# Attention scores copied to SBUF by the maximum, masks one and transposes two iterations later

## The chip, the cores and the metric

One core of a Trainium2 chip. The metric is the device time of one execution in microseconds (us), the median of three runs of the kernel before: 988.97 (988.1 to 991.67). Engines: PE is TensorE, PEld its weight load, DVE is VectorE, ACT is ScalarE, POOL is GpSimd, SP issues most DMAs.

## The reference, cut to what matters

```
scores = scale * q @ k.T                      # 4 batches x 8 heads, 576 x 576, head size 64
thresh = max(scores, axis=-1) - tau
scores = where(scores >= thresh, scores, -1e9)
attn = exp(scores - max(scores)); attn /= sum(attn) + 1e-9
x = (attn @ v) as [2304, 512]
e = argmax(x @ w_gate + bias); x = gate * (relu(x @ w1[e]) @ w2[e])   # 8 experts, one per token
h = x @ w_in; out = (h * sigmoid(1.702 h)) @ w_out
```

Only the attention is touched by the change.

## The kernel before, in words

The attention works on 16 pairs of heads (4 per batch). A pair is 9 units: unit w < 8 is 128 query rows of one head, unit 8 holds the last 64 rows of both heads. So there are 144 units, and `run` makes two of them in each iteration; nine iterations are two pairs.

Of one unit, in the old code:

- `qk` (L201 to L217): four (unit 8: eight) matmuls on TensorE give scores of 128 x 576 in a PSUM tile `sc`, of which there are two. K and Q are split into a high and a low part, and operand tiles hold both.
- `max` (L219 to L226): a TENSOR_REDUCE on VectorE over `sc` gives the negated maximum `nmx`.
- `thr` (L228 to L232): threshold from `nmx`, on VectorE, from iteration 66 on GpSimd.
- `exp` (L234 to L238): ScalarE, from `sc` in PSUM.
- `mask` (L240 to L271): SCALAR_TENSOR_TENSOR on VectorE: `sc >= thr` times `e`, with the row sum accumulated, into `E`. After unit 8 of every second pair come four small steps for the reciprocals.
- `trans` (L274 to L297): four transposes on TensorE, and a copy on ScalarE to `AT`. `trans_tails` does the last 64 columns.
- `av_items`: 10 pieces for each pair, matmuls with V; `row_items`: 5 pieces for every second pair, which turn the result into rows, scale them on GpSimd (`xrow`, `lgt`) and write them out.

An iteration `it` does units 2it and 2it+1 from `qk` to `mask` and the transposes of the two units before. Each engine takes its work in the order in which it is written. Tables (`AV`, `ROW`, `AVL`, `ROWL`) say how many pieces of `avq` and `rowq` go into an iteration, `sides` puts steps of the router in between, and from iteration 54 (`IT_LAST`) on these steps also stand between the masks.

Operands of pair p+2 are made while pair p runs: `load` (DMA of K and Q), then two pieces of `split` (L144 to L154), one for each iteration, on GpSimd: scale the query half, cast to the high part `kA`, subtract for the low part `kB`. After the second, `place` copies halves of the tiles on the SP queue: four DMAs (L161 to L164).

Of the kernel before, what the change touches and what calls it, by code (L numbers as in the profile page):

```python
# [24 lines left out]
UPP = 9  # L25
# [7 lines left out]
NS0 = 7  # L33
CO = (0, 2)
CA = (0, 1, 2, 2, 2, 2, 2, 2, 2, 2, 2, 2, 2, 2, 2, 2)
# [6 lines left out]
NROW = 2  # L42
IT_THR = 66
SN = 1
# [3 lines left out]
class Attention:  # L48
# [12 lines left out]
    def __init__(self, ctx, late_ctx, tc, kq, v, tau, w_gate, x_dram, router, ident, ps):  # L61
# [9 lines left out]
        self.kp = P("a_k", 3)  # L71
        self.ep = P("a_e", 4)
        self.ex = P("a_exp", 3)
        self.et = P("a_et", 2)
        self.sm = P("a_small", 4)
        router.wk["A"] = P("r_work_a", 1)
# [13 lines left out]
        self.w_gate = w_gate  # L90
        self.qT = [cst.tile([128, 1536], F32R, name=f"qT{i}") for i in range(3)]
        for t in self.qT:
# [39 lines left out]
    def operands(self, p):  # L132
        d = self.st[p]
        d["qT"] = self.qT[p % 3]
        for x in ("kA", "kB"):
            d[x] = self.kp.tile([128, 1536], F32R, name=x)

# [5 lines left out]

    def split(self, p, i, pieces):  # L144

        nc = self.nc
        d = self.st[p]
        n = 640 // pieces
        A, B_, F = (self.heads(d[x], n, i * n) for x in ("kA", "kB", "F"))
# [68 lines left out]

    def max(self, u):  # L219
        nc = self.nc  # L220
        p, w = divmod(u, UPP)
        d = self.st[p]
        sc = d["sc", w]
# [4 lines left out]
    def thr(self, u, eng):  # L228
        p, w = divmod(u, UPP)
        d = self.st[p]  # L230
        d["thr", w] = thr = self.sm.tile([128, 1], F32, name="thr")
        eng.tensor_scalar(thr, d["nmx", w], -1.0, self.taue[:, 0:1], op0=ALU.mult, op1=ALU.subtract)  # L232

    def exp(self, u):  # L234
        p, w = divmod(u, UPP)
        d = self.st[p]
        d["e", w] = e = self.ex.tile([128, 2, 288], F32, name="e")
        self.nc.scalar.activation(e, d["sc", w][:, :, 0:288], ACTF.Exp, bias=d["nmx", w][:, 0:1], scale=1.0)  # L238

    def mask(self, u):  # L240
# [17 lines left out]
        else:  # L258
# [132 lines left out]
    def run(self):  # L391
# [15 lines left out]
        while done < NU:  # L407
            last = it >= IT_LAST
            us = [u for u in (2 * it, 2 * it + 1) if u < NU]
            ts = [u for u in (2 * it - 2, 2 * it - 1) if 0 <= u < NU]  # L410
            starts = [u // UPP for u in us if u % UPP == 0]
            for p in starts:
                if p + 3 < NPAIR:
                    self.load(p + 3)
                if p + 2 < NPAIR:
                    self.load_v(p + 2)
                for n in range(1 if p == 0 else p + 2, min(p + 3, NPAIR)):
                    self.operands(n)
                    self.poolq += [lambda n=n, i=i: self.split(n, i, NPC) for i in range(NPC)]
            thr_eng = nc.gpsimd if it >= IT_THR else nc.vector  # L420
            copies = []
            for i in range(2):
# [4 lines left out]
                if i == 0 and not last:  # L427
                    n = AV1[it % 9]
                    while n and avq:
                        avq.pop(0)()  # L430
                        n -= 1
            for i in range(2):
                for c in range(2):
                    if CO[c] == 2 * i and c < len(copies):
                        copies[c]()
                if i < len(us):
                    self.max(us[i])
                    self.exp(us[i])
                for c in range(2):
                    if CO[c] == 2 * i + 1 and c < len(copies):  # L440
                        copies[c]()
# [10 lines left out]
            n = AVL[it - IT_LAST] if last else AV[it % 9]  # L452
# [5 lines left out]
            n = ROWL[it - IT_LAST] if last else ROW[it % 9]  # L458
# [999 lines left out]
```

## Time and profile before

| what | us |
|---|---|
| median of three runs | 988.97 (988.1 to 991.67) |
| the profiled execution, own time | 989.85 |
| its span, first to last instruction | 988.1 |
| TensorE busy in the span | 932.2 (94%) |
| VectorE busy | 568.2 (58%) |
| ScalarE busy | 440.2 (45%) |
| GpSimd busy | 241.6 (24%) |
| first score matmul, last score matmul | 7.6, 311.7 |

The attention is the first third, from 7.6 to about 320 us; the experts and the last layer follow. Busy shares of the span are means over these stages. In the views, a line's "idle" is the time its engine stood still just before it, and behind the arrow stands what ended it.

### The profile page before, as it was taken

To read this page: it belongs to the slowest core of one execution; us is meant where nothing else is said; L and a number is where in the kernel's file an instruction comes from. 1 tells how busy PE (TensorE), PEld (TensorE's weight loads), DVE (VectorE), ACT (ScalarE), POOL (GpSimd) and SP (SyncE) were. 2 spreads that over 40 slices of the span, in tenths; PEclk is the share of its full clock that TensorE was granted. 3 is DMA by queue.
4 is the path that set the end of the run, shared out by engine and by line. 5 is a ranking of instruction groups with operands and counts; after the bars stand their busy time and mean duration, and the time that the engine had idled before them with its cause. 6 is when DMAs were issued, how large, how long until landed. Compare 5 with 4: busy or idle time off the path is not lost. (4 is left out here: it accounts for less than half of the span.)

```text
span 988.1 us, 14131 instructions
## 1 busy us (share of the span) xinstructions
PE 932.2 (94%) x4991; PEld 747.5 (76%) x4991; DVE 568.2 (58%) x1182; ACT 440.2 (45%) x799; POOL 241.6 (24%) x338
## 2 busy tenths in 40 slices
PE   5799899999987989999999999999999999999994
PEld 4677677777765668777788888888888888888894
DVE  6698999898886387676777569971111111111110
ACT  4567677777665434343444434542222222222221
POOL 5735565666415332020222010010001000100100
PEclk9899999999999999999999999999999999999998
DMA  6766645655504426545645224330011000100000
GB/s 181 176 169 182 147 126 132 155 139 125 125 9 115 149 69 199 193 159 175 204 166 190 72 86 150 106 107 23 1 44 43 1 0 22 43 1 1 33 11 24
DMA packets 78571, 100.08 MB, mean 101 GB/s; under 512 B 28639, under 2 KB 51679, under 8 KB 78496
## 3 DMA queue, kind: packets, MB, share of 16 engines
q1 hardware_dynamic: 74656, 86.63, 30.9%
q0 software_dynamic: 3840, 12.50, 3.8%
q8 instruction: 41, 0.67, 0.3%
q14 instruction: 34, 0.28, 0.1%
HBM read 63.46 MB, written 17.23 MB: 82 GB/s over the span
## 5 line engine op out<-in xcount | busy, mean ns | idle before, releaser
L1154 DVE TENSOR_TENSOR hl<-sg,hh 128x512 fp32r<-128x512 f32 (+1 forms) x80 | 51.0, 638 | 243.1 <-ACT hh L1152 240.4
L1151 ACT ACTIVATE sg<-tr 128x512 f32<-128x512 f32 (+1 forms) x80 | 44.2, 553 | 208.6 <-PE tr L938 205.2
L214 PE MATMUL sc<-kA,qT 128*128 128x288 f32 x320 | 105.5, 346 | 25.4 <-DVE thr L232 8.0
L225 DVE TENSOR_REDUCE nmx<-sc 128x1 f32<-128x576 f32 x144 | 108.4, 753 | 22.1 <-PE sc L214 20.5
L938 PE MATMUL tr<-xh,wi_h 128*128 128x512 f32 (+1 forms) x320 | 120.6, 377 | 0.0
L938 PE MATMUL tr<-xh,wi_l 128*128 128x512 f32 (+1 forms) x320 | 118.8, 371 | 0.0
L938 PE MATMUL tr<-xl,wi_h 128*128 128x512 f32 (+1 forms) x320 | 118.7, 371 | 0.0
L238 ACT ACTIVATE e<-sc,nmx 128x576 f32<-128x576 f32 x144 | 108.0, 750 | 18.4 <-DVE nmx L225 18.1
L960 PE MATMUL sc<-wo_h,hl 128*128 128x512 f32 x288 | 113.8, 395 | 0.0
L960 PE MATMUL sc<-wo_l,hh 128*128 128x512 f32 x288 | 113.7, 395 | 0.0
L960 PE MATMUL sc<-wo_h,hh 128*128 128x512 f32 x288 | 113.5, 394 | 0.0
L262 DVE SCALAR_TENSOR_TENSOR E<-sc,thr,e 128x576 f32<-128x576 f32 x128 | 104.3, 815 | 12.2 <-ACT e L238 8.2
L291 ACT COPY AT<-tr 128x512 f32<-128x512 f32 x128 | 75.0, 586 | 61.1 <-PE tr L289 59.4
L214 PEld LDWEIGHTS sc<-kA,qT 128*128 128x128 f32 x320 | 62.5, 195 | 45.5 <-issue 25.5
L214 PE MATMUL sc<-kB,qT 128*128 128x288 f32 x320 | 92.8, 305 | 1.2 <-DMA kB<-kB 1.1
L289 PE MATMUL tr<-ident,E 128*128 128x128 f32 x512 | 79.7, 280 | 0.2 <-DVE E L262 0.2
L335 PE MATMUL av<-AT,V 128*64 128x288 f32 x512 | 77.0, 420 | 0.0
L938 PEld LDWEIGHTS tr<-xh,wi_l 128*128 128x128 f32 x320 | 60.2, 188 | 11.3
L938 PEld LDWEIGHTS tr<-xl,wi_h 128*128 128x128 f32 x320 | 60.3, 188 | 11.2
L938 PEld LDWEIGHTS tr<-xh,wi_h 128*128 128x128 f32 x320 | 60.2, 188 | 11.2
L960 PE MATMUL sc<-bl,hh 128*128 128x512 f32 x152 | 60.1, 395 | 6.5 <-DVE bl L1179 6.5
L289 PEld LDWEIGHTS tr<-ident,E 128*128 128x128 f32 x512 | 65.0, 145 | 0.8 <-DVE E L262 0.7
(213 smaller groups left out, 1757.3 us busy)
## 6 DMA issues: line engine op xcount, KB each, us to landing
ra<-in_moe_w_dram SPq DMA_DIRECT2D x20, 512.0 KB, 5.2
rb<-in_moe_w_dram SPq DMA_DIRECT2D x20, 512.0 KB, 3.9
F<-in_kq_dram SPq DMA_DIRECT2D x15, 640.0 KB, 5.4
cv_raw<-in_moe_w_in_dram SPq DMA_DIRECT2D x16, 512.0 KB, 4.8
cv_raw<-in_moe_w_out_dram SPq DMA_DIRECT2D x16, 512.0 KB, 3.9
kA<-kA SPq DMA_DIRECT2D x15, 320.0 KB, 3.3
kB<-kB SPq DMA_DIRECT2D x15, 320.0 KB, 3.5
x_dram<-xrow SPq DMA_DIRECT2D x72, 64.0 KB, 2.1
```

Source lines behind the costliest of these rows:

```text
L214: nc.tensor.matmul(sc[:, hf, 0:288], l, d[kk][:, c0 + hf * 288:c0 + (hf + 1) * 288], start=(i == 0), stop=(i == len(ops) - 1),)
L225: nc.vector.tensor_reduce(out=nmx, in_=sc[:, :, 0:288], axis=AX.XY, op=ALU.max, negate=True)
L238: self.nc.scalar.activation(e, d["sc", w][:, :, 0:288], ACTF.Exp, bias=d["nmx", w][:, 0:1], scale=1.0)
L262: nc.vector.scalar_tensor_tensor(out=E.rearrange("p (a c) -> p a c", a=2), in0=d["sc", w][:, :, 0:288], scalar=d["thr", w][:, 0:1], in1=d[ ...
L289: nc.tensor.transpose(tp[:, kc * 128:(kc + 1) * 128], E[:, k0 + kc * 128:k0 + (kc + 1) * 128], self.ident)
L291: copies.append(lambda: nc.scalar.copy(AT[:, h, :, c * 128:(c + 1) * 128], tp.rearrange("p (k c) -> p k c", k=4)))
L335: nc.tensor.matmul(d["av"][h * 64:(h + 1) * 64, 0:288], d["V"][:, h, kc, :], d["AT"][:, h, kc, hf * 288:(hf + 1) * 288], start=False, stop ...
L938: nc.tensor.matmul(hps[:, 0:T], w[:, kd, :], blk[x][:, kd, :], start=(i == 0), stop=(i == 11))
L960: nc.tensor.matmul(y, h[:, cs], w, start=(f == 0 and i == 0), stop=(f == blk["nf"] - 1 and i == 2))
L1151: nc.scalar.activation(sg, hps, ACTF.Gelu_apprx_sigmoid)
L1154: return [upper, lambda: nc.vector.tensor_sub(hl, sg, hh.bitcast(F32))]
```

## The change

- `max` is a TENSOR_SCALAR on VectorE: it writes the negated scores to an SBUF tile `ns` (three of them) and accumulates the minimum of these, which is `nmx`. `exp` and `mask` read `ns` (with the sign turned), and no longer `sc`.
- `thr` is on GpSimd always.
- An iteration does `qk`, `max`, `exp` and `thr` of units 2it and 2it+1, `mask` of the two units before these, and transposes of the two units before those. VectorE's order is mask, maximum, mask, maximum. The tables are read one iteration later (`jt`).
- `split` becomes `high` (scale and cast, GpSimd) and `low` (subtract, VectorE), queued as high, high, low, low, one for each iteration (two in iteration 0). `place` follows the second `low`.
- `load_v` of pair p+2 is issued when unit 0 of pair p is transposed, two iterations later than before.
- One more `E` tile, six instead of four of the small tiles, operand tiles of 1408 instead of 1536 columns.

The core of the diff:

```diff
-    def split(self, p, i, pieces):
+    def high(self, p, i, pieces):
+        nc = self.nc
+        d = self.st[p]
+        n = 640 // pieces
+        A, F = (self.heads(d[x], n, i * n) for x in ("kA", "F"))
+        nc.gpsimd.tensor_scalar_mul(F[64:128], F[64:128], self.cq[64:128, 0:1])
+        nc.gpsimd.tensor_copy(A, F)
+
+    def low(self, p, i, pieces):
         d = self.st[p]
         n = 640 // pieces
         A, B_, F = (self.heads(d[x], n, i * n) for x in ("kA", "kB", "F"))
-        nc.gpsimd.tensor_scalar_mul(F[64:128], F[64:128], self.cq[64:128, 0:1])
-        nc.gpsimd.tensor_copy(A, F)
-        nc.gpsimd.tensor_sub(B_, F, A.bitcast(F32))
+        self.nc.vector.tensor_sub(B_, F, A.bitcast(F32))
         if i == pieces - 1:
             self.place(p)
...
-        nc.vector.tensor_reduce(out=nmx, in_=sc[:, :, 0:288], axis=AX.XY, op=ALU.max, negate=True)
-        d["nmx", w] = nmx
+        ns = self.sn.tile([128, 2, 288], F32, name="ns")
+        nc.vector.tensor_scalar(
+            ns, d["sc", w][:, :, 0:288], -1.0, 3.0e38, op0=ALU.mult, op1=ALU.min, accum_out=nmx)
+        d["nmx", w], d["ns", w] = nmx, ns
...
-        eng.tensor_scalar(thr, d["nmx", w], -1.0, self.taue[:, 0:1], op0=ALU.mult, op1=ALU.subtract)
+        self.nc.gpsimd.tensor_scalar(thr, d["nmx", w], self.taue[:, 0:1], None, op0=ALU.add)
...
-        self.nc.scalar.activation(e, d["sc", w][:, :, 0:288], ACTF.Exp, bias=d["nmx", w][:, 0:1], scale=1.0)
+        self.nc.scalar.activation(e, d["ns", w], ACTF.Exp, bias=d["nmx", w][:, 0:1], scale=-1.0)
...
-            out=E.rearrange("p (a c) -> p a c", a=2), in0=d["sc", w][:, :, 0:288],
-            scalar=d["thr", w][:, 0:1], in1=d["e", w], op0=ALU.is_ge, op1=ALU.mult, accum_out=acc,
+            out=E.rearrange("p (a c) -> p a c", a=2), in0=d["ns", w],
+            scalar=d["thr", w][:, 0:1], in1=d["e", w], op0=ALU.is_le, op1=ALU.mult, accum_out=acc,
...
-            last = it >= IT_LAST
-            us = [u for u in (2 * it, 2 * it + 1) if u < NU]
-            ts = [u for u in (2 * it - 2, 2 * it - 1) if 0 <= u < NU]
+            jt = it - 1
+            last = jt >= IT_LAST
+            us, ms, ts = ([u for u in (2 * n, 2 * n + 1) if 0 <= u < NU] for n in (it, it - 1, it - 2))
...
-                if p + 2 < NPAIR:
-                    self.load_v(p + 2)
                 for n in range(1 if p == 0 else p + 2, min(p + 3, NPAIR)):
                     self.operands(n)
-                    self.poolq += [lambda n=n, i=i: self.split(n, i, NPC) for i in range(NPC)]
+                    self.poolq += [lambda n=n, i=i, f=f: f(n, i, NPC) for f in (self.high, self.low) for i in range(NPC)]
...
             for i in range(2):
-                for c in range(2):
-                    if CO[c] == 2 * i and c < len(copies):
-                        copies[c]()
+                if i < len(copies):
+                    copies[i]()
+                if i < len(ms):
+                    self.mask(ms[i])
+                if last:
+                    self.sides(SD[i], False)
                 if i < len(us):
                     self.max(us[i])
                     self.exp(us[i])
...
-                if i == 0 and us:
-                    self.thr(us[0], thr_eng)
-                if last:
-                    self.sides(SD[i], False)
-            for i, u in enumerate(us):
-                if i:
-                    self.thr(u, thr_eng)
-                self.mask(u)
+                    self.thr(us[i])
...
-            n = 1
+            n = 1 if it else 2
             while n and self.poolq:
```

How the order changes on VectorE, in the regular part of the attention. One iteration before (`nmx<-sc` is the maximum, `thr` the threshold, `E` the masked result):

```order
L225 TENSOR_REDUCE nmx<-sc 128x1
L232 TENSOR_SCALAR thr<-nmx,taue 128x1
L225 TENSOR_REDUCE nmx<-sc 128x1
L262 SCALAR_TENSOR_TENSOR E,rs<-sc,thr,e 128x576
L232 TENSOR_SCALAR thr<-nmx,taue 128x1
L262 SCALAR_TENSOR_TENSOR E,rs<-sc,thr,e 128x576
```

And one iteration of the change with a subtraction at its end (`ns` is the copy of the scores), with the first instruction of the next:

```order
L268 SCALAR_TENSOR_TENSOR E,rs<-ns,thr,e 128x576
L230 TENSOR_SCALAR ns,nmx<-sc 128x576
L268 SCALAR_TENSOR_TENSOR E,rs<-ns,thr,e 128x576
L230 TENSOR_SCALAR ns,nmx<-sc 128x576
L156 TENSOR_TENSOR kB<-F,kA 128x2x320
L268 SCALAR_TENSOR_TENSOR E,rs<-ns,thr,e 128x576
```

The masks stand ahead of the maxima of their iteration, since they belong to the units before; thresholds are gone, the subtraction is new.

How it changes on GpSimd, in the same part. Before (`F`, `kA`, `kB` are the operands, `xrow` and `lgt` a row step):

```order
L373 TENSOR_TENSOR xrow<-xr,r 128x256
L378 TENSOR_TENSOR lgt<-xr,r 128x32
L150 TENSOR_SCALAR F<-F,cq 64x2x320
L151 CAST kA<-F 128x2x320
L152 TENSOR_TENSOR kB<-F,kA 128x2x320
L373 TENSOR_TENSOR xrow<-xr,r 128x256
L378 TENSOR_TENSOR lgt<-xr,r 128x32
```

And now:

```order
L238 TENSOR_SCALAR thr<-nmx,taue 128x1 x2
L379 TENSOR_TENSOR xrow<-xr,r 128x256
L384 TENSOR_TENSOR lgt<-xr,r 128x32
L149 TENSOR_SCALAR F<-F,cq 64x2x320
L150 CAST kA<-F 128x2x320
L238 TENSOR_SCALAR thr<-nmx,taue 128x1 x2
L379 TENSOR_TENSOR xrow<-xr,r 64x256
```

Two thresholds open each iteration there, and stand behind the row and operand steps of the iteration before.

## Rows read from the trace of the kernel before

**Rows 1.** Windows by stage: window, its length, busy us of each engine, clock, DMA.
```profile
core 0: us, PE busy (x) PEld busy (x) DVE busy (x) ACT busy (x) POOL busy (x), PEclk, DMA share, GB/s
38.69:97.97 59.28, 57.72 (x415) 44.09 (x416) 52.95 (x129) 43.45 (x88) 27.98 (x36) 1.00 0.66 170
97.97:129.39 31.42, 28.07 (x200) 21.62 (x200) 28.63 (x74) 20.33 (x41) 16.42 (x28) 1.00 0.57 130
129.39:164.90 35.51, 34.85 (x257) 27.35 (x256) 32.34 (x83) 26.61 (x54) 20.88 (x24) 1.00 0.57 140
164.90:231.37 66.47, 65.12 (x476) 51.13 (x475) 60.56 (x152) 50.53 (x102) 41.75 (x49) 1.00 0.61 147
231.37:309.70 78.33, 72.53 (x508) 55.64 (x506) 66.67 (x184) 51.87 (x107) 33.88 (x61) 0.96 0.30 71
```

**Rows 2.** Waits of TensorE, 38.69 to 309.7 us: total us, times, longest.
```profile
PE sc L214 <- DVE E L262: 6.2, 8, 1.9
```

**Rows 3.** VectorE's groups, 129.39 to 164.9: count, busy us, mean ns, idle before.
```profile
L262 DVE SCALAR_TENSOR_TENSOR E<-sc,thr,e 128x576 f32<-128x576 f32 x17 | 13.9, 817 | 1.7 <-ACT e L238 1.6
L225 DVE TENSOR_REDUCE nmx<-sc 128x1 f32<-128x576 f32 x18 | 13.6, 753 | 1.3 <-PE sc L214 1.1
L232 DVE TENSOR_SCALAR thr<-nmx,taue 128x1 f32<-128x1 f32 x18 | 3.8, 211 | 0.3
L262 DVE DVE_READ_ACCUMULATOR E<-sc,thr,e 128x1 f32 x16 | 1.3, 83 | 0.0
```

**Rows 4.** Timeline of VectorE: start us, duration; first masks of two iterations.
```profile
41.62 0.81 DVE L262 SCALAR_TENSOR_TENSOR E<-sc,thr,e 128x576 f32<-128x576 f32 x1
45.11 0.81 DVE L262 SCALAR_TENSOR_TENSOR E<-sc,thr,e 128x576 f32<-128x576 f32 x1
```

**Rows 5.** VectorE's groups over the whole span: two SBUF operands, GpSimd idle.
```profile
L198 DVE TENSOR_TENSOR kB<-F,kA 128x640 fp32r<-128x640 f32 x2 | 1.6, 810 | 0.0
L195 DVE SCALAR_TENSOR_TENSOR qT<-F,cq,qT 64x576 fp32r<-64x576 f32 x2 | 1.6, 808 | 0.1
```

**Rows 6.** Timeline of VectorE and GpSimd at three places where they meet.
```profile
172.33 1.89 POOL L150 TENSOR_SCALAR F<-F,cq 64x640 f32<-64x640 f32 x1
173.03 0.20 DVE L651 TENSOR_TENSOR v<-v,m 128x40 f32<-128x40 f32 x1
...
176.73 1.89 POOL L150 TENSOR_SCALAR F<-F,cq 64x640 f32<-64x640 f32 x1
176.95 0.64 DVE L653 TENSOR_TENSOR oh<-v,valid 128x40 bf16<-128x40 f32 x1
...
298.16 0.69 POOL L373 TENSOR_TENSOR xrow<-xr,r 128x256 f32<-128x256 f32 x1 [1.54 <-ACT xr L370]
298.30 1.23 DVE L838 TENSOR_TENSOR OL<-iota,plf 128x640 bf16<-128x640 f32 x1
```

**Rows 7.** Line 838 by itself: shortest, median and longest duration in ns.
```profile
L838 DVE TENSOR_TENSOR OL<-iota,plf x6: 807/1026/3078, 298.3 to 364.5; 128x640 bf16<-128x640 f32 x5, 128x1280 bf16<-128x1280 f32 x1
```

**Rows 8.** GpSimd's groups, 129.39 to 164.9 us.
```profile
L150 POOL TENSOR_SCALAR F<-F,cq 64x640 f32<-64x640 f32 x4 | 7.6, 1889 | 0.4
L152 POOL TENSOR_TENSOR kB<-F,kA 128x640 fp32r<-128x640 f32 x4 | 6.2, 1551 | 0.3
L151 POOL CAST kA<-F 128x640 fp32r<-128x640 f32 x4 | 2.9, 716 | 0.3
L373 POOL TENSOR_TENSOR xrow<-xr,r 128x256 f32<-128x256 f32 x4 | 2.5, 613 | 14.2 <-ACT xr L370 10.1 <-DMA V<-in_v_dram 4.0
L378 POOL TENSOR_TENSOR lgt<-xr,r 128x32 f32<-128x32 f32 x4 | 1.0, 239 | 0.0
```

**Rows 9.** Thresholds on GpSimd, 100 to 310 us (from iteration 66 on).
```profile
L232 POOL TENSOR_SCALAR thr<-nmx,taue 128x1 f32<-128x1 f32 x10 | 3.5, 353 | 16.4 <-DVE nmx L225 13.1 <-DVE end L740 3.3
```

**Rows 10.** Waits of GpSimd, 38.69 to 309.7 us: total us, times, longest.
```profile
POOL xrow L373 <- DMA x_dram<-xrow: 7.4, 1, 7.4
```

**Rows 11.** Timeline of the SP queue: first and last of a pair's four operand copies.
```profile
153.15 0.63 SPq L161 DMA_DIRECT2D qT<-kA  x1
...
158.01 0.59 SPq L164 DMA_DIRECT2D kB<-kB  x1
```

More of the change, by code (lines that the diff above doesn't have):

```diff
@@ L42 @@
 NROW = 2
-IT_THR = 66
 SN = 1
@@ L71, in __init__ @@
         self.kp = P("a_k", 3)
-        self.ep = P("a_e", 4)
+        self.ep = P("a_e", 5)
         self.ex = P("a_exp", 3)
+        self.sn = P("a_neg", 3)
         self.et = P("a_et", 2)
-        self.sm = P("a_small", 4)
+        self.sm = P("a_small", 6)
         router.wk["A"] = P("r_work_a", 1)
@@ L90, in __init__ @@
         self.w_gate = w_gate
-        self.qT = [cst.tile([128, 1536], F32R, name=f"qT{i}") for i in range(3)]
+        self.qT = [cst.tile([128, 1408], F32R, name=f"qT{i}") for i in range(3)]
         for t in self.qT:
@@ L135, in operands @@
         for x in ("kA", "kB"):
-            d[x] = self.kp.tile([128, 1536], F32R, name=x)
+            d[x] = self.kp.tile([128, 1408], F32R, name=x)
     def heads(self, t, n, c=0, r=None):
@@ L148, in split @@
         n = 640 // pieces
-        A, B_, F = (self.heads(d[x], n, i * n) for x in ("kA", "kB", "F"))
+        A, F = (self.heads(d[x], n, i * n) for x in ("kA", "F"))
         nc.gpsimd.tensor_scalar_mul(F[64:128], F[64:128], self.cq[64:128, 0:1])
         nc.gpsimd.tensor_copy(A, F)
-        nc.gpsimd.tensor_sub(B_, F, A.bitcast(F32))
+    def low(self, p, i, pieces):
+        d = self.st[p]
+        n = 640 // pieces
+        A, B_, F = (self.heads(d[x], n, i * n) for x in ("kA", "kB", "F"))
+        self.nc.vector.tensor_sub(B_, F, A.bitcast(F32))
         if i == pieces - 1:
@@ L222, in max, with thr @@
         d = self.st[p]
-        sc = d["sc", w]
         nmx = self.sm.tile([128, 1], F32, name="nmx")
-        nc.vector.tensor_reduce(out=nmx, in_=sc[:, :, 0:288], axis=AX.XY, op=ALU.max, negate=True)
-        d["nmx", w] = nmx
-    def thr(self, u, eng):
+        ns = self.sn.tile([128, 2, 288], F32, name="ns")
+        nc.vector.tensor_scalar(
+            ns, d["sc", w][:, :, 0:288], -1.0, 3.0e38, op0=ALU.mult, op1=ALU.min, accum_out=nmx)
+        d["nmx", w], d["ns", w] = nmx, ns
+    def thr(self, u):
         p, w = divmod(u, UPP)
@@ L414, in run @@
                     self.load(p + 3)
-                if p + 2 < NPAIR:
-                    self.load_v(p + 2)
                 for n in range(1 if p == 0 else p + 2, min(p + 3, NPAIR)):
                     self.operands(n)
-                    self.poolq += [lambda n=n, i=i: self.split(n, i, NPC) for i in range(NPC)]
-            thr_eng = nc.gpsimd if it >= IT_THR else nc.vector
+                    self.poolq += [lambda n=n, i=i, f=f: f(n, i, NPC) for f in (self.high, self.low) for i in range(NPC)]
+            for u in ts:
+                if u % UPP == 0 and u // UPP + 2 < NPAIR:
+                    self.load_v(u // UPP + 2)
             copies = []
@@ L438, in run @@
                     self.exp(us[i])
-                for c in range(2):
-                    if CO[c] == 2 * i + 1 and c < len(copies):
-                        copies[c]()
-                if i == 0 and us:
-                    self.thr(us[0], thr_eng)
-                if last:
-                    self.sides(SD[i], False)
-            for i, u in enumerate(us):
-                if i:
-                    self.thr(u, thr_eng)
-                self.mask(u)
+                    self.thr(us[i])
                 if last:
                     self.sides(SD[i + 2], False)
-            n = AVL[it - IT_LAST] if last else AV[it % 9]
+            n = AVL[jt - IT_LAST] if last else AV[jt % 9]
             while n and avq:
@@ L457, in run @@
                 self.trans_tails(u)
-            n = ROWL[it - IT_LAST] if last else ROW[it % 9]
+            n = ROWL[jt - IT_LAST] if last else ROW[jt % 9]
             while n and rowq:
```

3 lines of the change are left out of this document (1 added, 2 removed).

## The prediction

> **What bounds the kernel now.** I read the stages first, then the waits, then one regular stretch in detail. In the attention stage [rows 1] TensorE is busy 57.72 of 59.28 us, 34.85 of 35.51 and 65.12 of 66.47 in the three regular windows. Two windows are looser: 97.97 to 129.39 us (28.07 of 31.42), where the routing tables are set up, and 231.37 to 309.70 us (72.53 of 78.33, at a mean granted clock of 0.96), where routing steps lie between the masks. The second thing to see in the same rows is VectorE: 32.34 of 35.51 us. So two engines are nearly full, and TensorE is the fuller one. What it waits for by name is mostly the mask [rows 2]: the score buffers (two) come free only when the mask has read them, and a score matmul stood 6.2 us in 8 waits for it. Behind the attention (from 310 us to the end) the change touches nothing, so I take that part as shifted.
>
> One regular iteration of VectorE [rows 4] runs from one first mask (41.62) to the next (45.11), 3.49 us; its durations add up to 2 x 0.82 + 2 x 0.75 + 2 x 0.21 + 2 x 0.08 = 3.7 [rows 3], so neighbours overlap by 0.2 us an iteration, 1.9 us in nine. Nine iterations (two head pairs) took 35.51 us, 3.95 each: most iterations are longer than VectorE's 3.49, which fits TensorE as the bound.
>
> **The change part by part**, per nine iterations (18 units), unless said otherwise.
>
> *Thresholds leave VectorE*: 18 x 0.211 = -3.8 us [rows 3]. They cost GpSimd 18 x 0.353 = 6.4 us [rows 9].
>
> *The maximum* becomes a TENSOR_SCALAR that also writes 576 values to SBUF and needs an accumulator read. No row has it. From below it costs the reduction's 0.753, from above the mask's 0.817, which reads the same PSUM data, writes as much and accumulates; I take the middle, 0.785, plus 0.083 for the read: 18 x (0.785 - 0.753 + 0.083) = +2.1 us (1.5 to 2.6).
>
> *The mask* reads two SBUF operands. The nearest row has the same operation with a per-partition scalar and two SBUF operands of 576: 0.808 [rows 5], against 0.817 now. I take no change.
>
> *The low halves* (four of `tensor_sub` on 128x640) come to VectorE at 0.81 each [rows 5]: +3.2 us. GpSimd loses 4 x 1.551 = 6.2 us [rows 8], so its load stays about the same (20.88 - 6.2 + 6.4 = 21.1 of 35.5).
>
> VectorE's sum: 32.34 - 3.8 + 2.1 + 3.2 = 33.8 us of durations, 31.9 without the overlap, where 30.4 stood before. **It is not relieved**; it has 3.6 us to spare in 35.5.
>
> *A collision that was not there.* With two SBUF operands VectorE meets GpSimd's reads. The rows show it: a 40-element operation that started 0.22 us after a GpSimd scaling took 0.64 us and ended 0.86 us after the scaling's start, but one that started 0.70 us after another scaling took 0.20, although the scaling went on for 1.0 us more [rows 6]. A 640-element one took 1.23 beside `xrow` [rows 6], against 0.807 alone [rows 7]: 0.42 lost, until 0.56 us after `xrow` began. So a GpSimd instruction holds VectorE up only in its first part: I take 0.86 us for a scaling and 0.56 for a cast and for `xrow`. An operation that starts at a random time then waits (4 x 0.86² + 9 x 0.56²) / (2 x 35.5) = 0.08 us; 18 masks and 4 subtractions lose 1.8 us (from below 0, if the starts never meet). From above, whole instructions hold: (4 x 1.889² + 4 x 0.716² + 5 x 0.613² + 18 x 0.353²) / 71 = 0.29 us each [rows 8, 9], 6.4 us in all. I take 1.8, by the 0.20 us row: VectorE then needs 33.7 of 35.5 us, still below TensorE.
>
> [...]
>
> *Who waits for whom.* A score buffer is now free after the maximum, not after exponential and mask, and transposes want masks of the iteration before. TensorE and VectorE can each run about one unit ahead; long and short iterations even out. What this can give back is TensorE's idle time [rows 1]: 3.6 us in the three regular windows, 3.35 in the setup window, 5.8 in the last one plus 0.04 x 78.33 = 3.1 us that the lower clock took there: 15.8 us, the ceiling. I take half of the first (1.8; both engines stay nearly full), 2.5 of the second (blocked VectorE steps there no longer hold the score buffers) and 5.7 of the last 8.9 (the longest wait on a mask, 1.9 us [rows 2], is of that kind): 10 us.
>
> *GpSimd's queue*: a threshold can start when its maximum is done and is wanted some 2.4 us later, at the mask of the next iteration (3.95 less 2 x 0.75). Where a step of the operands (1.89 + 0.72) and a row step stand before it, it comes later than that; VectorE's lead over TensorE covers about a unit of it. Cost taken: 0; from above it is a rival below.
>
> *SP's queue*: V loads are issued two iterations later, used in the next pair: covered. The four copies of the operands come after the second subtraction, two to three iterations later, and their issues span 153.15 to 158.60 [rows 11]; the pair needs them about five iterations (20 us) on. Only pair 2 at the start has a margin near zero: 1 us taken (0 to 3). One more iteration at the end: 1 us taken (0 to 3.5, [rows 4]).
>
> *ScalarE* reads the scores from SBUF; it is busy 26.61 of 35.51 us [rows 1], so 18 exponentials could each be 0.4 us longer before it fills. Cost 0.
>
> **Sum**: -10 + 2 = -8 us. The profiled execution's own time is 989.85, so 981.9; the median shown is 0.9 below that execution, so **981.0 us**.
>
> **The rivals.** *No room*: TensorE is full as it is, the idle time that is given back in some places is lost at both ends. For it: 1.35 us idle in 66.47 [rows 1]. It gives 985 to 991, say 987.
>
> *The collision takes whole instructions* (slower). Place: each mask. VectorE needs 31.9 + 6.4 = 38.3 us in nine iterations, 2.8 more than now; 271 / 35.5 = 7.6 such stretches: +21 us, less the gains outside the regular windows: about 1002. It decides once the wait per mask passes 0.16 us (3.6 / 22). For it: the 1.23 us row; against it: the 0.20 us row.
>
> [...]
>
> *Thresholds come late.* In two of nine iterations a row step (0.613 + 0.239 of `lgt`) and an operand step precede one: 3.5 us against 2.4, so up to 1.1 us each, 2.2 x 7.6 = 17 us from above; and `xrow` once waited 7.4 us for its buffer's DMA [rows 10], which would now stop masks too. TensorE's slack takes part of it: about 993.
>
> **How the numbers follow.** The forecast has 0.48, no room 0.27, late thresholds 0.10, whole instructions 0.10, two passes 0.05. What a measurement here can tell from no change is about 0.5%, 4.9 us: the forecast is faster by more; no room and 0.04 of the late thresholds are within it: 0.48, 0.31, 0.21. The ceiling of 15.8 with some luck at the start gives 970; above, the range takes in late thresholds and part of the collision: 1000. The likeliest case's own range is 974 to 984.
>
> **What would show it.** Right: the TENSOR_SCALAR near 0.79, the mask near 0.81 with some at 1.2 to 1.6, the subtraction near 0.81; TensorE's waits no longer on the mask but on the maximum, in small amounts; the last window with a clock nearer 1. Wrong: a mean mask above 1.0, VectorE waiting on `thr` from GpSimd by several us in all, or a regular stretch of nine iterations longer than 35.5 us.

## The result and the profile after

The changed kernel takes 1003.98 us (1000.45 to 1004.24) against 989.15 us (988.1 to 991.67) for the kernel before: 1.0134 times, 95% interval 1.0109 to 1.0158. Forecast was 981.0; it is **slower by 1.3%**. The profiled execution is the fastest of the four, 1000.45, so its 10.6 us against the profiled one of before are the lower end of the loss.

First the stages, cut at the same iterations as [rows 1] (first score matmul of iterations 6, 21, 28, 37, 54, 71):

```profile
core 0: us, PE busy (x) PEld busy (x) DVE busy (x) ACT busy (x) POOL busy (x), PEclk, DMA share, GB/s
33.78:97.72 63.94, 57.49 (x406) 43.64 (x405) 54.26 (x140) 45.57 (x88) 43.89 (x62) 1.00 0.60 153
97.72:130.01 32.29, 28.21 (x194) 20.91 (x194) 26.92 (x76) 20.42 (x39) 23.17 (x42) 1.00 0.52 118
130.01:167.87 37.86, 36.11 (x258) 27.41 (x256) 33.45 (x87) 26.94 (x53) 27.54 (x37) 1.00 0.70 167
167.87:238.65 70.78, 67.78 (x486) 51.79 (x484) 61.09 (x163) 51.26 (x101) 55.13 (x77) 1.00 0.55 132
238.65:311.62 72.97, 69.17 (x493) 52.27 (x491) 61.54 (x186) 50.80 (x105) 44.44 (x78) 1.00 0.34 79
```

Iteration 6 starts at 33.78 instead of 38.69, iteration 71 at 311.62 instead of 309.70. With the start of the first expert matmul (328.31 before, 337.78 now) the whole account is:

| stage | before | after | difference |
|---|---|---|---|
| start to iteration 6 | 38.69 | 33.78 | -4.9 |
| 6 to 21 | 59.28 | 63.94 | +4.7 |
| 21 to 28 (setup) | 31.42 | 32.29 | +0.9 |
| 28 to 37 | 35.51 | 37.86 | +2.4 |
| 37 to 54 | 66.47 | 70.78 | +4.3 |
| 54 to 71 (last window) | 78.33 | 72.97 | -5.4 |
| 71 to the first expert matmul | 18.61 | 26.16 | +7.6 |
| the rest of the span | 659.79 | 660.92 | +1.1 |

These differences must be read with care, because the cuts are at score matmuls, and in the changed kernel the transposes, the av work and the routing steps stand one iteration later against the scores. A cut there leaves more work behind it. Before iteration 6 TensorE has done 32 of the transposes of L295, where it had done 40 of the same (L289). The routing matmuls began 2.1 us ahead of iteration 71 and now begin 4.0 us behind it (before, then after: count, durations in ns, first and last start):

```profile
L857 PE MATMUL tr<-R,OL x35: 169/206/216, 307.6 to 379.3; 128*128 128x96 bf16 x20, 128*128 128x16 bf16 x15
```
```profile
L856 PE MATMUL tr<-R,OL x35: 169/206/216, 315.6 to 390.0; 128*128 128x96 bf16 x20, 128*128 128x16 bf16 x15
```

So neither the 4.9 at the start nor the 5.4 of the last window is time won as it stands. Up to iteration 21 it is 97.72 us against 97.97, no difference; in iterations 21 to 54 7.5 us are lost; from iteration 54 to the first expert matmul it is 99.13 us against 96.94, 2.2 us more. The start scatters, too: in three kernels below that do the same up to there, iteration 6 starts at 35.24, 35.55 and 37.14. And the last line of the table is not the same in all kernels: below, the rest lies between 658.7 and 664.3, which is as much as the effects at the end, and what sets it stays open.

The window of 28 to 37 shows where to look: VectorE is busy 33.45 of 37.86, so neither it nor TensorE (36.11) is full, and GpSimd has gone from 20.88 to 27.54. What VectorE waits for, iterations 6 to 71 (total us, times, longest):

```profile
DVE E L268 <- POOL thr L238: 27.9, 21, 4.0
DVE ns L230 <- PE sc L218: 6.5, 8, 1.8
```

27.9 us on thresholds, where the waits of TensorE on masks in [rows 2] were 6.2. VectorE's operations cost nearly what was worked out. Its groups and then GpSimd's, 130.01 to 167.87 (count, busy us, mean ns, idle before), against [rows 3] and [rows 8, 9]:

```profile
L230 DVE TENSOR_SCALAR_CACHE_REDUCE ns<-sc 128x576 f32<-128x576 f32 x19 | 14.1, 744 | 0.3 <-PE sc L218 0.3
L268 DVE SCALAR_TENSOR_TENSOR E<-ns,thr,e 128x576 f32<-128x576 f32 x16 | 14.0, 877 | 4.0 <-POOL thr L238 3.9
L268 DVE SCALAR_TENSOR_TENSOR ET<-ns,thr,e 128x576 f32<-128x576 f32 x2 | 2.5, 1238 | 0.0
L156 DVE TENSOR_TENSOR kB<-F,kA 128x640 fp32r<-128x640 f32 x4 | 3.8, 953 | 0.0
```
```profile
L238 POOL TENSOR_SCALAR thr<-nmx,taue 128x1 f32<-128x1 f32 x18 | 10.9, 608 | 7.4 <-DVE ns L230 7.2
L149 POOL TENSOR_SCALAR F<-F,cq 64x640 f32<-64x640 f32 x4 | 8.1, 2033 | 0.4
```

The maximum takes 744 ns although it writes 576 values more than the reduction's 753; the mask 877 here, and 1238 the two of unit 8 (`ET`); the low half 953. The threshold is the surprise: 608 ns on GpSimd (353 in [rows 9]), and it stands in a queue. This is one late threshold, GpSimd and VectorE in order of start:

```profile
131.54 0.75 DVE L230 TENSOR_SCALAR_CACHE_REDUCE ns<-sc 128x576 f32<-128x576 f32 x1
...
132.12 0.61 POOL L379 TENSOR_TENSOR xrow<-xr,r 128x256 f32<-128x256 f32 x1 [0.36 <-ACT xr L376]
...
132.70 0.75 POOL L384 TENSOR_TENSOR lgt<-xr,r 128x32 f32<-128x32 f32 x1
...
133.55 1.90 POOL L149 TENSOR_SCALAR F<-F,cq 64x640 f32<-64x640 f32 x1
...
135.52 0.72 POOL L150 CAST kA<-F 128x640 fp32r<-128x640 f32 x1
...
136.21 0.54 POOL L238 TENSOR_SCALAR thr<-nmx,taue 128x1 f32<-128x1 f32 x2
...
136.52 0.82 DVE L268 SCALAR_TENSOR_TENSOR E<-ns,thr,e 128x576 f32<-128x576 f32 x1 [2.48 <-POOL thr L238]
```

The maximum that starts at 131.54 is done at 132.29. Its threshold stands behind a row step (`xrow`, `lgt`), a scaling and a cast, which began at 132.12 and end at 136.24; two thresholds then run, and the mask that wants the first of them, with 2.48 us idle before it, starts at 136.52. In iteration 71 and behind, the rows that matter are these (SBUF copy `xT` and the cast `ah` on ScalarE, the matmul that wants `xT`, and the index step that everything of the routing chain leads to):

```profile
317.33 0.18 DVE L872 TENSOR_SCALAR igaA<-ixs 128x8 int32<-128x8 f32 x1
...
327.99 1.04 ACT L1177 CAST ah<-ra 128x1024 fp32r<-128x1024 f32 x1 [3.20 <-DMA ra<-in_moe_w_dram]
328.94 0.39 ACT L346 COPY xT<-av 128x288 f32<-128x288 f32 x1
...
329.38 0.85 PE L337 MATMUL av<-ATt,Vt 128*128 128x288 f32 x1 [3.91 <-ACT xT L346]
```

The step that writes `igaA` starts 5.7 us after iteration 71 does; in the kernel before it started at 309.27, 0.4 us ahead of that iteration. ScalarE's cast waits 3.20 us for the first expert weight, and `xT` stands behind it, so TensorE is idle for 3.91 us (1.59 at this place before). And the clock falls:

```profile
325.50:329.38 3.88, 0.00 (x0) 0.00 (x0) 0.31 (x1) 1.34 (x2) 0.18 (x1) 0.99 0.98 305
329.38:333.00 3.62, 3.62 (x12) 1.71 (x14) 0.91 (x1) 0.04 (x1) 0.22 (x1) 0.54 0.94 340
```

### The profile page after: what moved, and what is told of

The parts are those of the page before. It is cut to its first block, busy times and chain, and to the rows that moved or that the text cites. A ratio compares the mean times of both kernels' runs of the same rounds, so it can differ in the third digit from the quotient of the medians.

```text
span 998.7 us, 14257 instructions
## 1 busy us (share of the span) xinstructions
PE 936.1 (94%) x4991; PEld 745.0 (75%) x4991; DVE 565.2 (57%) x1224; ACT 444.1 (44%) x799; POOL 288.9 (29%) x440
## 5 line engine op out<-in xcount | busy, mean ns | idle before, releaser
L244 ACT ACTIVATE e<-ns,nmx 128x576 f32<-128x576 f32 x144 | 112.1, 778 | 85.4 <-DVE ns L230 82.5
L268 DVE SCALAR_TENSOR_TENSOR E<-ns,thr,e 128x576 f32<-128x576 f32 x128 | 108.6, 849 | 31.2 <-POOL thr L238 31.1
L230 DVE TENSOR_SCALAR_CACHE_REDUCE ns<-sc 128x576 f32<-128x576 f32 x144 | 107.6, 747 | 9.4 <-PE sc L218 9.2
L238 POOL TENSOR_SCALAR thr<-nmx,taue 128x1 f32<-128x1 f32 x144 | 82.8, 579 | 84.7 <-DVE ns L230 79.0
L295 PE MATMUL tr<-ident,E 128*128 128x128 f32 x512 | 78.4, 276 | 5.0 <-ACT AT L297 1.9
L297 ACT COPY AT<-tr 128x512 f32<-128x512 f32 x128 | 74.0, 578 | 13.8 <-PE tr L295 13.5
L295 PEld LDWEIGHTS tr<-ident,E 128*128 128x128 f32 x512 | 62.1, 141 | 8.9 <-ACT AT L297 3.5
L937 PEld LDWEIGHTS tr<-xh,wi_h 128*128 128x128 f32 x320 | 60.2, 188 | 11.2
```

What stands on the lines that cost most here:

```text
L230: nc.vector.tensor_scalar(ns, d["sc", w][:, :, 0:288], -1.0, 3.0e38, op0=ALU.mult, op1=ALU.min, accum_out=nmx)
L238: self.nc.gpsimd.tensor_scalar(thr, d["nmx", w], self.taue[:, 0:1], None, op0=ALU.add)
L244: self.nc.scalar.activation(e, d["ns", w], ACTF.Exp, bias=d["nmx", w][:, 0:1], scale=-1.0)
L268: nc.vector.scalar_tensor_tensor(out=E.rearrange("p (a c) -> p a c", a=2), in0=d["ns", w], scalar=d["thr", w][:, 0:1], in1=d["e", w], op0= ...
L295: nc.tensor.transpose(tp[:, kc * 128:(kc + 1) * 128], E[:, k0 + kc * 128:k0 + (kc + 1) * 128], self.ident)
L297: copies.append(lambda: nc.scalar.copy(AT[:, h, :, c * 128:(c + 1) * 128], tp.rearrange("p (k c) -> p k c", k=4)))
```

## The experiments

The theory after this reading: the loss in iterations 6 to 54 comes from thresholds that are late in GpSimd's queue, the loss at the end from a chain that the change shifted by one iteration. Rivals: VectorE is full with copies, low halves and held-up masks; the delay by an iteration is the cost; the transposes of the last units set the end. All edits are to the changed kernel unless said otherwise.

**The threshold on VectorE.**

```diff
-        self.nc.gpsimd.tensor_scalar(thr, ...
+        self.nc.vector.tensor_scalar(thr, ...
```

> The changed kernel with the threshold put back on VectorE, all else as changed. Theory (late thresholds in the regular part, and one iteration more before the routing steps at the end): the masks no longer wait for GpSimd (27.9 us in 21 waits between 30 and 330 us now), a nine-iteration stretch falls from 37.2 to 37.9 us to 35.5 to 36.0, iteration 54 starts at about 229 instead of 238.7, and the time is 992 to 995; the last part, from iteration 54 to the first expert matmul, does not get shorter. Rival (VectorE is full, its low halves and copies are the cost): 18 x 0.21 = 3.8 us more on VectorE per stretch, the stretch stays at 37 us or above, the time at 1001 to 1006.

Measured: 999.67 us, ratio 1.0095 (1.0061 to 1.0129). Between the two. Iteration 54 starts at 234.46 (after: 238.65; before: 231.37), and no wait for thresholds is left, but the stretches are 36.57 and 36.37. The window shows why:

```profile
128.64:165.21 36.57, 35.48 (x258) 27.26 (x256) 35.64 (x106) 27.15 (x54) 17.13 (x19) 1.00 0.72 172
```

VectorE is busy 35.64 of 36.57 us, and in iterations 6 to 54 it waits for scores only 1.3 us in all. The late thresholds are gone and VectorE is full instead: each side was half right. The first expert matmul stays at 337.18, so the end did not get shorter, as expected.

**The threshold on ScalarE**, which neither queue has.

```diff
-        self.nc.gpsimd.tensor_scalar(thr, d["nmx", w], self.taue[:, 0:1], None, op0=ALU.add)
+        self.nc.scalar.activation(thr, d["nmx", w], ACTF.Identity, bias=self.taue[:, 0:1], scale=1.0)
```

> The changed kernel with the threshold on ScalarE, behind the exponential. Neither GpSimd's queue nor VectorE has it; ScalarE gets 18 x 0.2 = 3.6 us in nine iterations and has 10 to spare. Theory (regular part lost to late thresholds; with them on VectorE it is VectorE's 3.8 us that kept the stretch at 36.4): the stretch falls to 35.0 to 35.7, iteration 54 starts at 228 to 231, the end is not mended, 990 to 995. Rival (the low halves and masks beside GpSimd's reads are what fills VectorE): stretch stays at 36.3 or above, time 998 or more.

Measured: 989.27 us, ratio 0.9987 (0.9969 to 1.0005). Windows at the same iterations:

```profile
36.19:94.66 58.47, 56.25 (x408) 43.53 (x406) 52.72 (x140) 49.85 (x118) 16.19 (x19) 1.00 0.61 158
94.66:125.57 30.91, 27.83 (x194) 20.90 (x194) 25.98 (x76) 22.27 (x53) 17.01 (x27) 1.00 0.58 136
125.57:160.94 35.37, 34.82 (x258) 27.27 (x256) 33.05 (x87) 30.25 (x71) 19.92 (x19) 1.00 0.75 179
160.94:227.24 66.30, 65.53 (x485) 51.59 (x484) 62.33 (x164) 57.87 (x136) 37.40 (x42) 1.00 0.59 141
227.24:298.52 71.28, 68.23 (x493) 52.33 (x491) 60.98 (x186) 56.48 (x139) 27.59 (x44) 1.00 0.35 81
```

The stretch is 35.37 (35.02 the next), with TensorE busy 34.82 and VectorE waiting 18.4 us for scores in iterations 6 to 71: TensorE is the bound again. Iterations 6 to 54 take 191.05 us, against 204.87 in the changed kernel and 192.68 before. So the place of one operation of 128 values costs 13.8 us there (11.4 by the start of iteration 54, 227.24 against 238.65). Without that loss the new order gives hardly anything back: two more kernels with this attention, below, take 192.51 and 190.59 for these iterations, and the kernel before takes 192.98 in the profile of its version with another order behind the loop. The last window is 71.28 and the last iteration starts 11.2 us earlier than in the kernel before, but the routing steps stand behind it here too: 28.08 us from there to the first expert matmul (326.60), and from iteration 54 to that matmul 99.36, against 96.94 before.

**Longer and shorter steps ahead of the threshold.** The low halves back on GpSimd, in one piece with scale and cast:

```diff
-        self.nc.vector.tensor_sub(B_, F, A.bitcast(F32))
+        self.nc.gpsimd.tensor_sub(B_, F, A.bitcast(F32))
```

> The changed kernel with the low halves back on GpSimd, in the same piece as scale and cast (as before the change). VectorE loses 4 x 0.92 = 3.7 us in nine iterations, GpSimd gets 4 x 1.55 = 6.2 us, and a piece of it is 4.3 us long instead of 2.8. Theory (late thresholds): masks wait longer for GpSimd, the stretch is 38.5 to 41 us, the time 1008 to 1025. Rival (VectorE's work is the cost): the stretch falls to 35.5 to 36.5, the time to 990 to 996.

Measured: 1034.81 us, ratio 1.0446 (1.0423 to 1.047); the stretch from iteration 28 is 41.60: the way that the theory had it, and beyond its range in both. And the operand step moved between the two thresholds of an iteration, away from the row step (the low halves on VectorE, which stand in the same list, move with it):

```diff
                     self.thr(us[i])
+                if i == 0:
+                    n = 1 if it else 2
+                    while n and self.poolq:
+                        self.poolq.pop(0)()
+                        n -= 1
...
-            n = 1 if it else 2
-            while n and self.poolq:
-                self.poolq.pop(0)()
-                n -= 1
```

> The changed kernel with the operand step (scale and cast, or the low half) written between the iteration's two thresholds instead of behind the row step, so that no threshold stands behind both. Theory (a threshold is late because a row step and an operand step, 4.0 us together, stand ahead of it in GpSimd's queue: 133.55 to 136.21 in the trace): the waits of masks for thresholds fall from 27.9 us (longest 4.0) to 5 to 15 us (longest 2.5), the stretch to 35.5 to 36.5, the time to 993 to 999. Rival (it is the load of GpSimd and the stretched thresholds, 0.79 us beside a mask, not what stands ahead): waits of 25 us or more, 1001 to 1006.

Measured: 999.06 us, ratio 1.0103 (1.0083 to 1.0123), just beyond what was expected, as are the stretch (36.74) and the waits; iteration 54 starts at 235.68. VectorE's waits for thresholds in the two kernels, iterations 6 to 71, the longer step first:

```profile
DVE E L268 <- POOL thr L238: 78.2, 27, 7.5
```
```profile
DVE E L268 <- POOL thr L238: 15.3, 28, 1.6
```

78.2 us with a longest of 7.5, 27.9 with 4.0, 15.3 with 1.6: the waits follow the length of what stands ahead in GpSimd's queue, in both directions. The time follows them, but by less: iterations 6 to 54 take 221.34, 204.87 and 201.76 us. That the threshold's place on GpSimd is the cause of the loss there is shown by the version with it on ScalarE, which has the whole 13.8 us back. How these divide between the steps ahead of a threshold and the stretched threshold itself is not settled: taking a part of the steps away gave 3.1.

**Without the delay by an iteration.** Masks in the iteration of their maxima, transposes one later, tables by `it`:

```diff
-            jt = it - 1
+            jt = it
-            us, ms, ts = (... for n in (it, it - 1, it - 2))
+            us, ms, ts = (... for n in (it, it, it - 1))
...
-                if i < len(ms):
-                    self.mask(ms[i])
...
+            for i in range(2):
+                if i < len(ms):
+                    self.mask(ms[i])
```

> The changed kernel with the iteration's structure of before: masks in the iteration of their maxima, transposes one later, tables not shifted; threshold still on GpSimd. Theory: the tail gets one iteration (4 us) back, but every mask now meets its threshold at once, so an operand step (2.08 + 0.72 us) or a row step (0.70 + 0.40) ahead of it on GpSimd holds a mask directly: the stretch grows to 38 to 40 us, the time is 1005 to 1018. Rival (the delay by an iteration is the whole cost, GpSimd does not matter): the stretch is 35.5, the time 989 to 993.

Measured: 1036.17 us, ratio 1.0473 (1.0452 to 1.0495), worse than either theory had it; the stretch is 44.73. VectorE's waits, iterations 6 to 71:

```profile
DVE E L268 <- POOL thr L238: 39.9, 18, 3.3
DVE E L268 <- ACT e L244: 23.0, 72, 0.8
```

In the iterations before the end the delay is not the cost, it hides part of it. The same with the threshold on VectorE:

> Both edits: threshold on VectorE and the iteration's structure of before. What is left of the change is the copy by the maximum and the low halves on VectorE. Theory: no wait for GpSimd, no shift at the end, but VectorE has 32.3 + 18 x 0.08 for the copy + 4 x 0.92 = 37.4 us of durations, 35.5 without the overlap of 1.9: a stretch of 35.5 to 36.5, and 987 to 995. Rival (VectorE's added work is the main cost): stretch above 37, time 1000 or more.

Measured: 1005.39 us, ratio 1.0168 (1.014 to 1.0196): the rival's number. The 35.5 of the theory came from durations of 37.4 less an overlap of 1.9, and VectorE's busy time alone is 37.85. What is left here is the copy and the low halves, in the old order, and VectorE is the bound with 37.85 of 39.66 us:

```profile
132.79:172.45 39.66, 35.83 (x258) 27.06 (x256) 37.85 (x108) 27.36 (x55) 16.14 (x20) 1.00 0.59 144
```

**The kernel before with the threshold on ScalarE**, ahead of the exponential (`taue` is made with the other sign), nothing else:

```diff
-        eng.tensor_scalar(thr, d["nmx", w], -1.0, self.taue[:, 0:1], op0=ALU.mult, op1=ALU.subtract)
+        self.nc.scalar.activation(thr, d["nmx", w], ACTF.Identity, bias=self.taue[:, 0:1], scale=-1.0)
...
+                    self.thr(us[i], thr_eng)
                     self.exp(us[i])
```

> The kernel before with nothing changed but the threshold, which goes from VectorE to ScalarE ahead of the exponential: VectorE loses 3.8 us in nine iterations. If TensorE bounds the old stretch, as the prediction had it: 35.3 to 35.6, time 985 to 990. If VectorE in truth bounds it (putting 5 us on it cost 4.1 us in each stretch): 32.5 to 34.5, time 965 to 982. If the threshold ahead of the exponential makes the exponentials late: above 36, 993 or more.

Measured: 999.8 us, ratio 1.009 (1.0055 to 1.0125); stretches 36.90 and 36.87. It is the third case: in the old order a mask wants its exponential at once, and VectorE waits for it (7.3 us in 40 waits in the kernel before, iterations 6 to 71):

```profile
DVE E L262 <- ACT e L238: 29.7, 69, 0.9
```

So thresholds on ScalarE, which the new order had room for (30.25 of 35.37 us busy with them), cost 1.4 us a stretch in the old one. The two edits are not quite alike: here the threshold stands ahead of the exponential, there behind it. That the distance between exponential and mask in the new order is what makes the room fits these waits, but no run here shows it by itself.

**The end: the tables.** One more av piece in iteration 67, and one iteration of pause instead of two ahead of the routing steps.

```diff
-AVL = (3, 2, 3, 3, 2, 3, 2, 3, 2, 3, 2, 3, 2, 3, ...
+AVL = (3, 2, 3, 3, 2, 3, 2, 3, 2, 3, 2, 3, 3, 3, ...
-NROW = 2
+NROW = 1
```

> The changed kernel with two numbers of its tables changed: one more piece of av work in iteration 67 (so that the last row pieces and what follows them come one iteration earlier) and a pause of one instead of two iterations between the last row piece and the routing steps. Theory (the end is set by the chain rows, routing steps, gathers, row stores, first expert weights, which the change shifted by one iteration): the indices igaA are ready 4 to 5 us earlier than at 317.3, the first expert matmul starts at 331 to 334 instead of 337.8, the time is 997 to 1000. Rival (the end is set by the transposes of the last units, which are one iteration later whatever the tables say): the first expert matmul stays at 337 to 338.5 and the time at 1002 to 1005.

> The threshold on ScalarE and the two table numbers together. Theory: the two gains add up, 985 to 991, at or below the kernel before. Rival (both act on one wait): no better than the better of the two alone, 992 or more.

Measured: 1005.46 (1.0166, 1.0129 to 1.0202) and 992.07 (1.0018, 1.0003 to 1.0034): no gain. The shift was undone (`igaA` starts 0.6 us ahead of iteration 71 in the first, 1.4 us in the second), but the last iteration itself came 8.5 and 9.9 us later than without the edit. The last window of the two, with the routing matmuls back in it:

```profile
239.50:320.14 80.64, 72.84 (x512) 55.30 (x510) 64.42 (x195) 53.23 (x110) 47.45 (x85) 0.96 0.33 77
```
```profile
228.93:308.44 79.51, 71.71 (x512) 55.04 (x510) 64.40 (x195) 58.71 (x143) 31.61 (x52) 0.96 0.36 83
```

It is as long as in the kernel before (78.33), at the same granted clock of 0.96, and the end behind it as short (18.60 and 17.76 us, 18.61 before). So the 5.4 us of the last window in the changed kernel were routing steps (and a row piece) that had left it, and the 7.6 at the end go with the same steps. In the second kernel a row matmul now stops TensorE in the middle of the scores:

```profile
299.99 0.70 PE L371 MATMUL tr<-G,xT 128*64 128x144 f32 x4 [4.00 <-ACT AT L297]
```

**The end: more routing steps in an iteration**, with av and row pieces where they were, alone and on top of the best version (further below).

```diff
-SD = (1, 2, 2, 2, 1)
+SD = (2, 3, 2, 2, 1)
```

> The changed kernel with ten instead of eight routing steps in each of the last iterations (SD 2, 3, 2, 2, 1 for 1, 2, 2, 2, 1), which pulls the routing chain about one iteration forward against the scores; av and row pieces stay where they are. Theory (the end is set by when the routing steps, and behind them gathers, row stores and weights, are done): igaA comes 4 to 6 us earlier against the last iteration than its 5.7 us behind it, the first expert matmul starts 2 to 5 us earlier than at 337.8, the time is 999 to 1002. Rival (the transposes of the last units set the end): 337 or later, 1002.5 to 1005.

> The same on top of the version with the threshold on ScalarE and the av pieces ahead of the first weight's cast (984.0). Theory: from the last iteration's first score matmul to the first expert matmul 20 to 23 us instead of 24.9, time 979 to 982. Rival: 24 to 25.5 us, 983 to 985, or more if the steps hold up the masks.

Measured: 1007.94 (1.0164, 1.0144 to 1.0183) and 990.71 (1.0, 0.9985 to 1.0014), the second worse than without the edit; the interval of the first overlaps that of the changed kernel (1.0109 to 1.0158). `igaA` again comes ahead of iteration 71, which again starts later (319.71 and 305.12). Here VectorE stops at a routing step that wants TensorE, with masks behind it:

```profile
301.41 0.17 DVE L864 TENSOR_SCALAR ixs<-tr 128x8 f32<-128x8 f32 x1 [4.03 <-PE tr L856]
```

So the routing steps' shift is real, and two ways to undo it gave back in the scores what they took from the end. That the transposes of the last units set the end is out for the ScalarE version at least: with the tables edited its last iteration came 9.9 us later and the first expert matmul stayed (326.20 against 326.60).

**The end: ScalarE's order.** Five av pieces ahead of the first weight's cast.

```diff
-    blocks[0]["split"](0, 0)
     att.tail(5)
+    blocks[0]["split"](0, 0)
```

> The kernel with the threshold on ScalarE, and after the loop five av pieces are written ahead of the first expert weight's cast instead of behind it, so that ScalarE's copy of xT no longer stands behind a cast that waits for the weight's DMA. Theory (a queue order that cost 1.6 us in the kernel before costs 4.7 us of TensorE's idle time now, because the row stores and the weight loads behind them come later against the transposes, and 5.8 us at a clock of 0.52 behind that): 4.7 + 5.8 / 2 = 7.6 at most, the first expert matmul starts at 319.5 to 322 instead of 326.6, the time is 982 to 985. Rival (the weights and the gathered rows set that start, the idle time is free): 325 to 327, and 988 to 990.

> The changed kernel with that same order after the loop and nothing else. Theory: 3.9 us idle and 3.6 us at a clock of 0.54 go, 3.9 + 1.7 = 5.6 at most: the first expert matmul starts at 332 to 334.5 instead of 337.8 and the time is 998 to 1000.5. Rival: 337 to 338, and 1003 to 1005.

> The kernel before with that same order after the loop: it has 1.6 us idle at this place and a clock of 1.00 behind it, so 0 to 1.6 us are to be had: 988 to 990, which a measurement cannot tell from no change. Rival (the order is worth the same in every kernel, so it is no loss of the change): 983 to 985.

Measured: 983.99 (0.9943, 0.9923 to 0.9963) on the version with the threshold on ScalarE, **the only one faster than the kernel before**; 1001.45 (1.0132, 1.0111 to 1.0153) on the changed kernel; 988.52 (1.0002, 0.9988 to 1.0017) on the kernel before, where it can't be told from no change. What the edit removes, in the ScalarE version without it (the matmul with what ended its wait, then the windows of the wait and behind it):

```profile
317.24 1.33 PE L337 MATMUL av<-ATt,Vt 128*128 128x288 f32 x2 [4.69 <-ACT xT L346]
```
```profile
312.50:317.24 4.74, 0.05 (x3) 0.00 (x1) 0.32 (x1) 1.34 (x2) 0.37 (x2) 0.86 0.96 307
317.24:323.00 5.76, 5.76 (x20) 2.67 (x22) 1.59 (x2) 0.63 (x2) 0.00 (x0) 0.52 0.26 99
```

With the edit the first expert matmul starts at 324.40, not at the 319.5 to 322 that I expected: TensorE now runs until it meets a gathered row that has not landed, and there is half the clock again behind that wait (0.50 from 319.50 to 321.50).

```profile
317.64 0.33 PE L921 MATMUL tr<-ident,xg 128*128 128x128 f32 x1 [1.74 <-DMA xg<-x_dram,igaA]
```

From the last iteration to the first expert matmul it is 24.9 us against 28.1. So the time came where it was expected, but not by the way that the theory had: that start is nearer to the rival's 325 to 327. Nor does the profile show where the gain comes from: it caught the slowest of the six executions (988.60), in which the 2.2 us won up to the first expert matmul are lost again behind it (the rest takes 662.4 us, 659.0 in the version without the edit). That the order helps is shown by the times, the way is not. The intervals of the two versions (0.9923 to 0.9963, 0.9969 to 1.0005) don't meet. On the changed kernel the profile shows a like gain (23.3 against 26.2), but the times, 1.0132 against 1.0134, don't show one outside their intervals.

## Why the prediction was wrong

**The step that failed first** is "GpSimd's queue: Cost taken: 0". The working held both numbers, 3.5 us of row and operand step ahead of a threshold that is wanted after 2.4, and then let "VectorE's lead over TensorE" take the difference. The trace has 4.0 us ahead, thresholds of 608 ns where 353 was taken (10.9 us in a stretch for 6.4), masks that wait 27.9 us, and 13.8 us lost in iterations 6 to 54 against the version without that queue. Two of the three signs named for a wrong forecast are there, the waits on `thr` and a stretch above 35.5. The rival "thresholds come late" (0.10) was the right one. Its bound from above, 17 us, was good; its forecast of 993 was not, since TensorE's slack took next to nothing: when a mask waits, the next maximum on VectorE waits behind it, and so does the score buffer (TensorE's waits for maxima are 7.9 us in 12, iterations 6 to 71).

**The second** is "What this can give back is TensorE's idle time": 10 us were taken, and next to nothing came. With the thresholds off GpSimd's queue the time is 0.9987 of that before (0.9969 to 1.0005), where 8 us less would be 0.992: so some 7 us of the miss are not the queue's. Of the last window 5.7 us were taken, 5.4 show in the table, and this nearness is luck. They are routing steps that went behind iteration 71, and with these put back the window takes 80.64 and 79.51 us at a clock of 0.96 again, against 78.33 before. In the regular and setup windows 4.3 was taken; iterations 6 to 54 without a late threshold take 190.59 to 192.51 us in three kernels, against 192.68 and 192.98 before, so about 1.5. There TensorE was full, as [rows 1] said. The rival "no room" (0.27) is the right one for this part, as far as the version without late thresholds shows it: its last iteration starts 11 us earlier, and its time is that of the kernel before.

**One more iteration at the end**, "1 us taken (0 to 3.5)": from iteration 54 to the first expert matmul the changed kernel takes 2.2 us more than the kernel before, and 2.4 more with the threshold on ScalarE, within that range. Of the two kernels with the threshold on VectorE the one with the delay takes 102.72 us there and the one without it 98.37. I had counted the masks and transposes of the last units and not the routing steps, which the tables shift by an iteration too, and the last iteration is 5.7 us long; behind them gathers, row stores and weight loads come later, and ScalarE's order and the lower clock add to it. How much each of these is worth is not settled: only the order was had separately, 3.2 and 2.9 us in the profiles of two pairs of kernels.

**VectorE's budget** was nearly right in its terms: the maximum 0.744 + 0.080 where 0.785 + 0.083 was taken (below the lower bound of 0.753), the mask's shortest and median time 0.803 and 0.815 over the whole span, against 0.817 in [rows 3] (so of two passes, given 0.05, nothing is seen), the held-up part 0.04 us a mask and 0.1 a subtraction over the whole span (0.10 and 0.14 in the stretch of the rows above), where 0.08 was taken, and below the 0.16 at which whole instructions would decide. Its sum, 31.9 + 1.8 = 33.7, stands against 33.45 measured, but two errors cancel in it. The 1.9 us "overlap" was taken off a number that has none in it, since a window's busy time counts overlapping instructions once: in that stretch the durations of the kernel before add up to 36.3 us, and 32.34 is what is left without the overlap. And the new operations were added with their whole durations, although they overlap with their neighbours as well. So VectorE had not 3.6 us to spare but about 2, as the run with the threshold on it shows (full at 36.6).

**The start**: 1 us lost was taken, and none is there: iteration 21 starts at 97.72 us, against 97.97. With the threshold on ScalarE it starts at 94.36 to 95.63 in three kernels, so 2 to 4 us are gained there, which I had not looked for. With the low halves back on GpSimd iteration 6 starts at 38.41 and iteration 21 at 105.76. That fits shorter operand steps on GpSimd as the reason, but the late thresholds are longer there too, and the cause stays open.

**ScalarE** at no cost was right: the exponential takes 0.778 from SBUF where it took 0.750, and even the thresholds find place there (30.25 of 35.37 us busy in the stretch with them, 26.94 of 37.86 without).

## What to carry to other kernels

An operation that costs 0.2 us is placed by what stands ahead of it in its queue, not by its own duration: before it goes to an engine that looks idle (GpSimd 24% busy over the span here, but 20.88 of 35.51 us in the regular stretch), add up the longest run of work that can stand in front of it, and compare that with the time until it is wanted. If the first is longer, the engine that waits in order stands still (VectorE here 27.9 us in 21 waits), and a third engine may have the place for nothing (ScalarE here). When an order is shifted by an iteration, list all that the same counter drives, the side steps and their loads too, and look at what the end of the loop waits for. Work that only moves across a cut looks like a gain in one stage and a loss in the next: check that the stages hold the same instructions before you read their difference.

## What was not expected of the hardware

GpSimd and VectorE again, from the other side. All thresholds of the changed kernel have one shape; they take from 272 to 1045 ns, half of them 783 or more. VectorE and GpSimd, in order of start:

```profile
146.62 0.81 DVE L268 SCALAR_TENSOR_TENSOR E<-ns,thr,e 128x576 f32<-128x576 f32 x1
146.78 0.79 POOL L238 TENSOR_SCALAR thr<-nmx,taue 128x1 f32<-128x1 f32 x1 [1.36 <-DVE ns L230]
...
148.03 0.75 DVE L630 TENSOR_REDUCE L<-lgt 128x40 f32<-128x320 f32 x1
...
148.20 0.28 POOL L238 TENSOR_SCALAR thr<-nmx,taue 128x1 f32<-128x1 f32 x1 [0.63 <-DVE ns L230]
...
148.58 1.90 POOL L149 TENSOR_SCALAR F<-F,cq 64x640 f32<-64x640 f32 x1
...
148.70 1.28 DVE L268 SCALAR_TENSOR_TENSOR ET<-ns,thr,e 128x576 f32<-128x576 f32 x1
```

Beside a reduction with one SBUF operand the threshold takes 0.28 us; beside a mask (two SBUF operands) it takes 0.79 and ends 0.14 us behind the mask. The mask that starts 0.12 us after a scaling takes 1.28 instead of 0.81, but ends 0.5 us before the scaling does. So the threshold that starts behind a mask lasts beyond the mask's end, and this mask, behind a scaling, does not last to the scaling's. The second operand in SBUF is what differs from before: the 144 masks of the kernel before, which read the scores from PSUM, take 792 to 820 ns, among them one that starts 0.19 us after a scaling (0.82 at 136.80); those of the changed kernel take 803 to 1281.

TensorE's mean granted clock was 0.52 for 5.8 us behind an idle time of 4.74 us, and 0.54 for 3.6 us behind 3.9 (0.50 up to 332.00 us, 1.00 again from 333.00 on); behind the 1.59 us of the kernel before it stayed at 1.00, but behind the 1.74 us wait for a gathered row it was 0.50. If TensorE bounds the time there, the first two waits cost about one and a half times their length, 7.5 and 5.5 us (an estimate: the idle time plus the share of the clock that was missing behind it). The order that removes them won 3.2 and 2.9 us up to the first expert matmul.
